# Transposing late tiles by DMA inside SBUF instead of on TensorE, with a new planned order and changed rings

## The chip, the cores and the metric

The kernel runs on 1 core of one Trainium2 chip. The metric is the device time of one execution in microseconds (us). Executions fall into a fast and a slow state; ratios and the conclusions from them use fast runs only, while a median with its range takes in the slow ones too. A ratio is the mean time of one kernel's fast runs over that of the other's of the same rounds on the same chip, so it is not quite the ratio of the medians quoted beside it. An interval after a ratio is its 95% interval. The kernel before has its own spread from chip to chip: its medians were 174.7 to 176.2 us.

## The reference, cut to what matters

```python
# attention: B=4, H=8, S=768, D=48
for t in range(S):
    cur = einsum('bhd,bhe->bhde', u[None] * kt, vt)
    y[:, :, t] = einsum('bhd,bhde->bhe', rt, state + cur)
    state = wt[..., None] * state + einsum('bhd,bhe->bhde', kt, vt)
x = y.transpose(0, 2, 1, 3).reshape(B, S, H * D)          # 4 x 768 x 384
# token mixing and a channel step
theta = x @ w_theta
y = w_tok_r @ (x * cos(theta)) + w_tok_i @ (x * sin(theta))
u = x + y
return u + maximum(u @ w_ch, 0)
```

A tile is 128 tokens of 384 channels. There are 24, numbered 0 to 23, six for each batch. Both `x @ w_theta` and `u @ w_ch` take the tile transposed (x^T, u^T), as the operand `lhsT` of TensorE's matmul.

## The kernel before

A planner orders all operations ahead of the run. It gives each operation an engine, a guessed duration and a priority, places them one by one, and so fixes the instruction stream of each engine. SP is the queue that issues the DMAs. What holds it delays every issue behind: below, the last load goes out at 142.42 us instead of 120.18. SBUF is the memory on the chip, PSUM the one that TensorE writes to. A ring is the number of buffers that the tiles of one name go through in turn.

```python
LAG = {"PE": 0.21, "ACT": 0.16, "DVE": 0.14, "POOL": 0.10, "SP": 1.5, "WQ": 2.5, "-": 0.0}
...
            for i, (eng, dur, fn, pen) in enumerate(o.alts):     # Planner.place
                t = max(free_at.get(eng, 0.0), t_slot)
                for d in o.deps:
                    t = max(t, d.end + (LAG[d.eng] if d.eng != eng else 0.0))
                if eng == "SP" and self.loads > 0:
                    t = max([free_at.get(eng, 0.0), t_slot and t_slot + self.slack[0]]
                            + [d.end + LAG[d.eng] + self.slack[1] for d in o.deps])
```

The end of a tile: TensorE mixes tokens, VectorE adds x, TensorE transposes u in three pieces into PSUM, ScalarE or VectorE copies u^T to SBUF, TensorE multiplies by `w_ch`, VectorE finishes, and SP stores.

```python
def f_ut():
    for j in range(NJ):                                   # NJ = 3
        nc.tensor.transpose(get(tx)[:, j, :], get(un)[:, j * L:(j + 1) * L], ident)
o_ut = P.op("PE", 0.17, f_ut, [o_un], [tx, uT], [], prio=-1.0, name=f"ut{b}{ti}")
...
o_uc = P.op("ACT", 0.38, f_uc, [o_ut], [], [tx], prio=-1.0, name=f"uc{b}{ti}",
            alts=[("DVE", 0.26, f_uc_v, PEN)])            # copy PSUM -> SBUF
def f_ml():
    for j in range(NJ):
        nc.tensor.matmul(get(ml), lhsT=get(uT)[:, j, :], rhs=wch[:, j, :], ...)
```

x^T is made in the same way. All loads and all output stores are issued on the SP queue.

## Time and profile before

| | |
|---|---|
| time | 174.72 us median (174.18 to 178.64, 3 runs) |
| profiled execution | span 175.3 us, state slow |
| TensorE (PE) busy in the span | 91% |
| TensorE busy from 128.6 to 171.9 us | 42.09 of 43.30 us |
| SP held by one 192 KB store | 0.34 us |

The prediction below shows how the page and its tables are read.

### The profile page before, as it was taken

The page shows a single profiled execution, that of the slowest core. Times are in us where ns is not written, and L with a number is a line of the kernel's source. Part 1 is how long each engine was busy: PE and PEld are TensorE (multiplying, and loading weights), DVE is VectorE, ACT ScalarE, POOL GpSimd, SP SyncE. Part 2 cuts the span into 40 slices and gives each one's busy share as a digit, 9 for nine tenths or more (in the row PEclk, how much of TensorE's full clock was granted, in tenths as well). Part 3 has the DMA queues.
Part 4 walks back from the last instruction along what each step waited for, and adds up shares of the span by engine and source line. Part 5 has one row for each costly group of instructions (what it writes and reads, how often), then busy time and mean ns, then how long its engine had stood idle before and what let it go on. Part 6 is the DMA issues. An engine that isn't in the chain of part 4 may idle for free.

```text
span 175.3 us, 4898 instructions
## 1 busy us (share of the span) xinstructions
PE 158.7 (91%) x1919; PEld 104.7 (60%) x1919; DVE 130.5 (74%) x278; ACT 117.7 (67%) x255; POOL 114.0 (65%) x134
## 2 busy tenths in 40 slices
PE   7699898999759999999977999999899999999980
PEld 7257565776536566776643667666566666566640
DVE  4507869797996899867899399869989884645461
ACT  2469689799996987966988049799986924810000
POOL 7388689989759578559799987999789310000000
PEclk9858699999996999999996599999999999999999
DMA  5999998899999999999999979989011012112212
GB/s 115 272 301 264 215 222 203 218 264 238 262 222 256 284 160 309 211 208 197 214 206 192 189 129 199 204 174 217 12 45 46 9 38 76 62 45 90 95 45 90
DMA packets 93768, 29.81 MB, mean 170 GB/s; under 512 B 88369, under 2 KB 92210, under 8 KB 93746
## 3 DMA queue, kind: packets, MB, share of 16 engines
q1 hardware_dynamic: 93344, 29.50, 75.9%
q8 instruction: 15, 0.25, 0.6%
q10 hardware_dynamic: 402, 0.00, 0.1%
q14 instruction: 7, 0.06, 0.1%
HBM read 24.78 MB, written 4.72 MB: 168 GB/s over the span
## 4 chain that ended last, share of the span: by engine, by line
PE 63%; DVE 12%; ACT 12%; DMA 8%; issue 1%; SPq 0%; ACTq 0%; DVEq 0%
PE bank L914 24%; DVE sb_z L891 7%; PE bank L941 6%; DMA sb_w<-in_moe_w_tok_i_dram 4%; PE cum L646 3%; PE bank L877 3%; DMA in_k<-in_k_dram 2%; DMA in_w<-in_w_dram 2%; PE bank L928 2%; PE bank L509 2%; PE bank L572 2%; ACT sb_a L439 2%; PE bank L491 2%; PE bank L493 2%; PE cum L430 2%; PE bank L593 1%
## 5 line engine op out<-in xcount | busy, mean ns | idle before, releaser
L914 PE MATMUL bank<-sb_z,wtokT 128*128 128x384 bf16 x288 | 56.3, 337 | 0.4 <-DVE sb_z L891 0.4
L914 PEld LDWEIGHTS <-wtokT 128*128 128x128 bf16 x288 | 27.2, 100 | 17.5 <-issue 3.2
L485 POOL TENSOR_TENSOR sb_bon<-sb_v,sb_rub 128x384 bf16<-128x384 bf16 x18 | 14.9, 829 | 15.0 <-ACT sb_v L465 8.4
L891 DVE TENSOR_TENSOR sb_z<-x_all,sb_sc 128x768 bf16<-128x768 bf16 x24 | 21.6, 911 | 2.4 <-ACT sb_sc L885 2.4
L923 DVE TENSOR_TENSOR sb_un<-bank,x_all 128x384 bf16<-128x384 f32 x24 | 13.3, 555 | 12.2 <-PE bank L914 12.1
L452 POOL TENSOR_TENSOR sb_k<-in_k,sb_a 128x384 bf16<-128x384 f32 x18 | 19.2, 1069 | 4.7 <-DMA in_k<-in_k_dram 4.7
L476 POOL TENSOR_TENSOR sb_ruk<-sb_ru,in_k 128x384 bf16<-128x384 f32 x18 | 19.2, 1067 | 0.6
L458 POOL TENSOR_TENSOR sb_q<-in_r,sb_a 128x384 bf16<-128x384 f32 x18 | 19.0, 1055 | 0.9 <-DMA in_r<-in_r_dram 0.9
L469 POOL TENSOR_TENSOR sb_ru<-in_r,u_bc 128x384 f32<-128x384 f32 x18 | 18.9, 1051 | 0.0
L439 ACT ACTIVATE sb_a<-cum 128x768 f32<-128x768 f32 x18 | 14.6, 810 | 6.0 <-PE cum L434 5.7
L326 ACT ACT_TABLE_LOAD x12 | 15.4, 1283 | 1.5 <-PEq L1025 1.3
L941 PE MATMUL bank<-wch,sb_uT 128*128 128x384 bf16 x72 | 15.7, 326 | 0.6 <-DVE sb_uT L935 0.6
L946 DVE SCALAR_TENSOR_TENSOR sb_o<-bank,sb_un 128x384 f32<-128x384 f32 x24 | 13.3, 553 | 3.9 <-PE bank L941 3.9
L882 ACT ACTIVATE sb_sc<-bank 128x384 bf16<-128x384 f32 x24 | 12.2, 510 | 4.1 <-PE bank L877 4.1
L932 ACT ACTIVATE sb_uT<-bank 128x384 bf16<-128x384 bf16 x16 | 7.8, 489 | 10.3 <-PE bank L928 10.1
L885 ACT ACTIVATE sb_sc<-bank,hpi 128x384 bf16<-128x384 f32 x24 | 14.6, 607 | 0.0
L877 PE MATMUL bank<-wth,sb_xT 128*128 128x384 bf16 x72 | 14.0, 326 | 0.4 <-DVE x_all L841 0.4
L497 DVE COPY sb_qkt<-bank 128x1024 bf16<-128x1024 bf16 x18 | 12.3, 683 | 1.3 <-PE bank L493 1.1
L514 DVE TENSOR_TENSOR sb_p<-bank,mask_exc 128x512 bf16<-128x512 f32 x18 | 12.3, 681 | 0.9 <-PE bank L509 0.8
L521 DVE TENSOR_TENSOR sb_p<-bank,mask_exc 128x512 bf16<-128x512 f32 x18 | 12.2, 679 | 0.0
L587 DVE TENSOR_TENSOR x_all<-bank,sb_bon 128x192 bf16<-128x192 f32 x36 | 10.9, 346 | 1.3 <-PE bank L572 1.3
L597 ACT ACTIVATE sb_xT<-bank 128x384 bf16<-128x384 bf16 x18 | 8.8, 495 | 4.3 <-PE bank L593 4.2
(131 smaller groups left out, 337.1 us busy)
## 6 DMA issues: line engine op xcount, KB each, us to landing
out_dram<-sb_o SPq DMA_DIRECT2D x24, 192.0 KB, 2.0
in_w<-in_w_dram SPq DMA_DIRECT2D x18, 192.0 KB, 5.3
in_r<-in_r_dram SPq DMA_DIRECT2D x18, 192.0 KB, 4.5
in_k<-in_k_dram SPq DMA_DIRECT2D x18, 192.0 KB, 4.5
in_v<-in_v_dram SPq DMA_DIRECT2D x18, 192.0 KB, 4.6
sb_w<-in_moe_w_tok_r_dram SPq DMA_DIRECT2D x6, 384.0 KB, 4.7
sb_w<-in_moe_w_tok_i_dram SPq DMA_DIRECT2D x6, 384.0 KB, 5.1
in_w<-in_w_dram SPq DMA_DIRECT2D x3, 384.0 KB, 5.1
```

Source lines behind the costliest of these rows:

```text
L326: nc.scalar.preload_act_table_set(name)
L439: nc.scalar.activation(get(a), get(cum)[:, :, :DM], AF.Exp)
L452: nc.gpsimd.tensor_tensor(get(kk)[:, :, :D], s["x_k"](), av(1), op=ALU.mult)
L458: nc.gpsimd.tensor_tensor(get(q)[:, :, :D], s["x_r"](), av(0), op=ALU.mult)
L469: nc.gpsimd.tensor_tensor(get(ru), s["x_r"](), u_bc, op=ALU.mult)
L476: nc.gpsimd.tensor_tensor(get(ruk), get(ru), s["x_k"](), op=ALU.mult)
L485: nc.gpsimd.tensor_tensor(get(bon), get(vb), get(rub).to_broadcast([L, H, D]), op=ALU.mult)
L877: nc.tensor.matmul(get(th), lhsT=get(s["xT"])[:, j, :], rhs=wth[:, j, :], start=(j == 0), stop=(j == NJ - 1))
L885: nc.scalar.activation(get(sc)[:, 0, :], get(th), AF.Sin, bias=hpi)
L891: nc.vector.tensor_tensor(get(zb[b])[:, c], xb, get(sc), op=ALU.mult)
L914: nc.tensor.matmul(get(ac), lhsT=wtokT[:, q_, s_, ti, :], rhs=get(zb[b])[:, s_, q_, :], start=(s_ == 0 and q_ == 0), stop=(s_ == NCH - 1 a ...
L941: nc.tensor.matmul(get(ml), lhsT=get(uT)[:, j, :], rhs=wch[:, j, :], start=(j == 0), stop=(j == NJ - 1))
```

## The change

The intent: TensorE alone sets the end, so take work from it. Six late x tiles (16 to 21) and eleven late u tiles (11 to 21) are transposed by DMA from SBUF to SBUF. That removes 51 transposes from TensorE and 17 copies from PSUM. Priorities and allocation penalties of the planner were retuned for it, and a few guessed durations changed.

```diff
+    XBAR = (11, 22)          # u tiles transposed by DMA
+    XBARX = (16, 22)         # x tiles
-    SLACK = (4.32, 5.23)
+    SLACK = (0.0, 5.53)
-    WIN = {'PE': 0.0, 'ACT': 0.0, 'DVE': 0.05, 'POOL': 0.56, 'SP': 0.12}
+    WIN = {'PE': 0.0, 'ACT': 0.02, 'DVE': 0.0, 'POOL': 0.19, 'SP': 0.0}
-             ... "sb_xT": 9, ... "sb_un": 3, "sb_uT": 3, ...
+             ... "sb_xT": 7, ... "sb_un": 4, "sb_uT": 4, ...
+        def f_ux():
+            for j in range(NJ):
+                nc.sync.dma_start(out=get(uT)[:, j, :], in_=get(un)[:, j * L:(j + 1) * L], transpose=True)
+        if XBAR[0] <= b * NCH + ti < XBAR[1]:
+            o_uc = P.op("SP", 0.9, f_ux, [o_un], [uT], [], prio=-1.0, name=f"ux{b}{ti}")
+        else:
+            (TensorE transpose and copy, as before)
     (the same for x^T with XBARX; planner durations: paired loads 1.46 -> 1.6, one state
      update 0.45 -> 0.76; the tables SHIFT and PENALTY, some 240 numbers, retuned: cut)
```

The planner takes three transposing DMAs for 0.9 us of SP and 1.5 us more until the data can be used.

More of the change, by code (lines that the diff above doesn't have):

```diff
@@ L59, in key @@
         num = name[len(kind):]
-        if kind in ("tok", "un", "ut", "uc", "ml", "fin", "st"):
+        if kind in ("tok", "un", "ut", "ux", "uc", "ml", "fin", "st"):
             b = int(num[0])
@@ L212 @@
     OFF = {'ln': -2.2, 'cum': -2.1, 'exp': -2.05, 'alt': -2.04, 'q': -1.5, 'k': -1.45, 'v': -1.2, 'ru': -1.3, 'ruk': -1.2, 'rub': -1.2, 'bon': -1.1, 'tqk': -0.9, 'qkt': -0.9, 'p': -0.8, 'm0': -0.7, 'pc': -0.7, 'sel': -1.6, 'y': -0.5, 'x': -0.5, 'xt': -0.4, 'xc': -0.4, 'rk': -1.3, 'rkt': -1.2, 'rkc': -1.2, 'beta': -1.15}
-    SHIFT = {'M': -0.23, 'M@0': 3.78, 'M@1': -3.52, 'M@3': 2.56, 'Mp@0': 0.29, 'S': -3.32, 'S@0': 0.3, 'S@1': -2.09, 'S@3': -3.9, 'Sp@0': -0.07, 'alt': -2.71, 'alt@0': -4.19, 'alt@1': -3.75, 'alt@3': -2.44, 'bc@0': -2.12, 'beta@0': 8.49, 'bon': -7.28, 'bon@0': -7.76, 'bon@1': -1.33, 'bon@3': -11.03, 'cos': -4.6, 'cos@0': -7.82, 'cos@1': -5.2, 'cos@3': -5.64, 'cum': 2.98, 'cum@0': -0.21, 'cum@1': 2.19, 'cum@3': 3.61, 'cump@0': -0.23, 'cwch': 2.19, 'cwch@1': 2.56, 'cwt': -0.63, 'cwt@1': -2.08, 'cwth': 0.26, 'cwth@1': -8.48, 'exp': -7.56, 'exp@0': -11.22, 'exp@1': -7.11, 'exp@3': -1.28, 'fin': 10.83, 'fin@0': 12.05, 'fin@1': 12.34, 'fin@3': 8.58, 'k': -2.66, 'k@0': -15.07, 'k@1': -5.34, 'k@3': -4.01, 'ldk': -0.07, 'ldk@0': 0.25, 'ldk@1': 0.06, 'ldk@3': 0.13, 'ldkp@0': -0.61, 'ldr': -0.52, 'ldr@0': -1.79, 'ldr@1': -0.84, 'ldr@3': -1.05, 'ldrp@0': -1.69, 'ldv': 0.27, 'ldv@0': 0.93, 'ldv@1': 1.13, 'ldv@3': 0.9, 'ldvp@0': 0.88, 'ldw': -1.63, 'ldw@0': -1.67, 'ldw@1': -1.98, 'ldw@3': -0.9, 'ldwp@0': -1.18, 'ln': -1.02, 'ln@0': -1.74, 'ln@1': -4.09, 'ln@3': 1.93, 'm': 1.57, 'm@0': 7.07, 'm@1': 11.91, 'm@3': 13.16, 'ml': 3.16, 'ml@0': -7.78, 'ml@1': -6.19, 'ml@3': -6.65, 'p': 4.22, 'p@0': 8.66, 'p@1': 14.26, 'p@3': 6.5, 'pc': 1.07, 'pc@0': 1.12, 'pc@1': -2.22, 'pc@3': -4.15, 'pp@0': 1.14, 'q': -0.33, 'q@0': -3.4, 'q@1': 0.28, 'q@3': 1.27, 'qkt': 1.93, 'qkt@0': -0.14, 'qkt@1': -5.68, 'qkt@3': -3.58, 'qktp@0': 2.71, 'rk@0': 6.13, 'rkc@0': 2.62, 'rkt@0': -1.07, 'ru': -2.75, 'ru@1': -1.4, 'ru@3': 2.61, 'rub': 1.54, 'rub@1': 3.53, 'rub@3': 6.25, 'ruk': -0.11, 'ruk@1': -0.56, 'ruk@3': 0.5, 'sel': 1.06, 'sel@0': 2.59, 'sel@1': -6.63, 'sel@3': -2.52, 'sin': 1.45, 'sin@0': 4.46, 'sin@1': -0.21, 'sin@3': 0.97, 'st': 0.43, 'st@0': -0.77, 'st@1': 3.72, 'st@3': -4.86, 'th': -5.14, 'th@0': -12.99, 'th@1': -9.62, 'th@3': -9.38, 'toE': -2.74, 'toE@0': -6.59, 'toE@1': -1.75, 'toE@3': -1.04, 'toS': -2.78, 'toS@0': 7.44, 'toS@1': 3.52, 'toS@3': 2.77, 'tok': -3.84, 'tok@0': -5.7, 'tok@1': -7.33, 'tok@3': -2.77, 'tqk': -0.37, 'tqk@0': -8.63, 'tqk@1': -1.82, 'tqk@3': -1.42, 'ubc': 3.86, 'ubc@1': 2.43, 'ublk@1': 8.43, 'ubm': 3.03, 'ubm@1': 3.71, 'uc': -4.81, 'uc@0': 3.89, 'uc@1': -2.11, 'uc@3': 5.25, 'un': 2.42, 'un@0': 2.75, 'un@1': -2.25, 'un@3': -1.11, 'ut': -3.32, 'ut@0': -2.56, 'ut@1': -8.44, 'ut@3': -9.24, 'v': 1.33, 'v@0': 5.45, 'v@1': 5.64, 'v@3': 6.18, 'wch': -0.56, 'wch@1': 1.93, 'wev': 2.67, 'wev@1': 6.99, 'wt': 0.86, 'wt@1': 0.73, 'wth': 0.4, 'wth@1': -1.64, 'wtr': 0.92, 'wtr@1': 2.77, 'x': 1.16, 'x@0': -4.58, 'x@1': 1.61, 'x@3': 1.76, 'xc': 1.62, 'xc@0': 2.07, 'xc@1': 3.0, 'xc@3': 1.78, 'xp@0': -0.04, 'xt': 0.48, 'xt@0': 1.96, 'xt@1': 3.17, 'xt@3': 6.63, 'y': -0.38, 'y@0': -2.78, 'y@1': -0.45, 'y@3': 0.21, 'yp@0': 1.15, 'z': -1.82, 'z@0': -4.53, 'z@1': -8.37, 'z@3': -5.1}
@@ L214 @@
-    PENALTY = {'S': 1.09, 'S@0': 1.12, 'S@1': 0.03, 'S@3': -0.59, 'bc@0': -1.6, 'bon@0': 0.89, 'cwch': -1.71, 'cwch@1': -0.3, 'cwt': 1.34, 'cwt@1': 1.64, 'cwth': 1.85, 'cwth@1': 2.85, 'k': 9.17, 'k@0': 6.71, 'k@1': 5.59, 'k@3': 6.89, 'pc': -1.22, 'pc@0': -2.79, 'pc@1': -4.83, 'pc@3': -6.18, 'qkt': 3.99, 'qkt@0': 1.6, 'qkt@1': 0.86, 'qkt@3': 2.34, 'qktp@0': 0.89, 'rk@0': 10.81, 'rkc@0': 2.27, 'ruk': -1.87, 'ruk@1': -3.89, 'ruk@3': -10.16, 'uc': 1.64, 'uc@0': 0.25, 'uc@1': 4.42, 'uc@3': -1.02, 'wev': -0.04, 'wev@1': 0.23, 'xc': -0.05, 'xc@0': 2.57, 'xc@1': 2.52, 'xc@3': 3.03, 'xp@0': 0.65}
+    SHIFT = {'M': -0.23, 'M@0': 3.78, 'M@1': -2.52, 'M@3': 3.01, 'Mp@0': 1.53, 'S': -3.32, 'S@0': 0.3, 'S@1': 0.63, 'S@3': -4.36, 'Sp@0': 1.4, 'alt': -2.71, 'alt@0': -4.47, 'alt@1': -1.63, 'alt@3': -4.6, 'bc@0': -1.23, 'beta@0': 12.08, 'bon': -7.28, 'bon@0': -5.29, 'bon@1': 0.35, 'bon@3': -8.1, 'cos': -4.6, 'cos@0': -9.33, 'cos@1': -3.49, 'cos@3': -3.96, 'cum': 2.98, 'cum@0': -0.21, 'cum@1': 3.75, 'cum@3': 5.42, 'cump@0': -1.49, 'cwch': 2.19, 'cwch@1': -0.96, 'cwt': -0.63, 'cwt@1': -3.12, 'cwth': 0.26, 'cwth@1': -9.29, 'exp': -7.56, 'exp@0': -10.19, 'exp@1': -4.56, 'exp@3': -1.55, 'fin': 10.83, 'fin@0': 10.99, 'fin@1': 9.97, 'fin@3': 7.33, 'k': -2.66, 'k@0': -18.8, 'k@1': -7.79, 'k@3': -6.46, 'ldk': -0.07, 'ldk@0': 0.25, 'ldk@1': 0.06, 'ldk@3': 0.42, 'ldkp@0': -0.45, 'ldr': -0.52, 'ldr@0': -1.79, 'ldr@1': -0.84, 'ldr@3': 0.67, 'ldrp@0': -0.91, 'ldv': 0.27, 'ldv@0': 0.93, 'ldv@1': 0.84, 'ldv@3': -0.27, 'ldvp@0': 0.3, 'ldw': -1.63, 'ldw@0': -1.67, 'ldw@1': -1.84, 'ldw@3': -0.9, 'ldwp@0': -1.25, 'ln': -1.02, 'ln@0': -1.36, 'ln@1': -1.33, 'ln@3': 6.49, 'm': 1.57, 'm@0': -0.46, 'm@1': 6.1, 'm@3': 7.68, 'ml': 3.16, 'ml@0': -6.91, 'ml@1': -8.02, 'ml@3': -8.42, 'p': 4.22, 'p@0': 8.66, 'p@1': 11.81, 'p@3': 4.5, 'pc': 1.07, 'pc@0': 1.12, 'pc@1': 0.19, 'pc@3': -5.32, 'pp@0': 1.11, 'q': -0.33, 'q@0': -4.36, 'q@1': -1.61, 'q@3': -1.63, 'qkt': 1.93, 'qkt@0': -0.16, 'qkt@1': -6.64, 'qkt@3': -4.47, 'qktp@0': 8.5, 'rk@0': 11.67, 'rkc@0': 2.6, 'rkt@0': 1.02, 'ru': -2.75, 'ru@1': 0.09, 'ru@3': 7.17, 'rub': 1.54, 'rub@1': 2.55, 'rub@3': 4.18, 'ruk': -0.11, 'ruk@1': -0.64, 'ruk@3': 0.54, 'sel': 1.06, 'sel@0': 2.59, 'sel@1': -8.51, 'sel@3': -0.48, 'sin': 1.45, 'sin@0': 8.03, 'sin@1': 7.28, 'sin@3': 7.7, 'st': 0.43, 'st@0': -3.12, 'st@1': -2.28, 'st@3': -8.52, 'th': -5.14, 'th@0': -11.38, 'th@1': -7.14, 'th@3': -9.55, 'toE': -2.74, 'toE@0': -3.59, 'toE@1': 4.98, 'toE@3': 1.37, 'toS': -2.78, 'toS@0': 8.07, 'toS@1': 9.18, 'toS@3': 4.18, 'tok': -3.84, 'tok@0': -3.56, 'tok@1': -5.9, 'tok@3': 0.22, 'tqk': -0.37, 'tqk@0': -7.79, 'tqk@1': -1.84, 'tqk@3': 1.63, 'ubc': 3.86, 'ubc@1': 2.17, 'ublk@1': 10.04, 'ubm': 3.03, 'ubm@1': -2.15, 'uc': -4.81, 'uc@0': 1.88, 'uc@1': -0.32, 'uc@3': 4.71, 'un': 2.42, 'un@0': 3.54, 'un@1': 0.59, 'un@3': 0.94, 'ut': -3.32, 'ut@0': 4.0, 'ut@1': -0.49, 'ut@3': -4.37, 'ux@1': 2.07, 'ux@3': 1.0, 'v': 1.33, 'v@0': 12.47, 'v@1': 13.27, 'v@3': 11.66, 'wch': -0.56, 'wch@1': 1.75, 'wev': 2.67, 'wev@1': 12.33, 'wt': 0.86, 'wt@1': 0.73, 'wth': 0.4, 'wth@1': -1.92, 'wtr': 0.92, 'wtr@1': 3.27, 'x': 1.16, 'x@0': -4.58, 'x@1': 1.58, 'x@3': 0.02, 'xc': 1.62, 'xc@0': 1.0, 'xc@1': 2.04, 'xc@3': -0.4, 'xp@0': -2.67, 'xt': 0.48, 'xt@0': 1.66, 'xt@1': 2.11, 'xt@3': 8.81, 'y': -0.38, 'y@0': -2.78, 'y@1': -1.02, 'y@3': -2.05, 'yp@0': 0.2, 'z': -1.82, 'z@0': 0.57, 'z@1': -4.1, 'z@3': -7.66}
@@ new lines @@
+    PENALTY = {'S': 1.09, 'S@0': 1.12, 'S@1': 0.25, 'S@3': -0.21, 'bc@0': -2.77, 'bon@0': 0.35, 'cwch': -1.71, 'cwch@1': -0.6, 'cwt': 1.34, 'cwt@1': 4.81, 'cwth': 1.85, 'cwth@1': 1.65, 'k': 9.17, 'k@0': 8.13, 'k@1': 8.89, 'k@3': 8.64, 'pc': -1.22, 'pc@0': -2.79, 'pc@1': -6.94, 'pc@3': -12.31, 'qkt': 3.99, 'qkt@0': 0.86, 'qkt@1': 3.26, 'qkt@3': 5.89, 'qktp@0': -1.33, 'rk@0': 9.44, 'rkc@0': 1.39, 'ruk': -1.87, 'ruk@1': -1.91, 'ruk@3': -13.18, 'uc': 1.64, 'uc@0': 1.43, 'uc@1': 5.04, 'uc@3': -1.26, 'wev': -0.04, 'wev@1': -0.16, 'xc': -0.05, 'xc@0': 2.47, 'xc@1': 2.67, 'xc@3': 2.65, 'xp@0': 0.98}
@@ L241 @@
              "sb_a": 3, "sb_alt": 5, "sb_v": 5, "sb_ru": 2, "sb_ruk": 2, "sb_rk": 2, "sb_rkT": 2, "beta": 1, "sb_rub": 2,
-             "sb_bon": 4, "sb_qkt": 4, "sb_p": 3, "sb_S": 3, "sb_SD": 3, "sb_xT": 9, "sb_sc": 3,
-             "sb_z": 3, "sb_w": 3, "sb_wn": 4, "sb_un": 3, "sb_uT": 3, "sb_o": 6}
+             "sb_bon": 4, "sb_qkt": 4, "sb_p": 3, "sb_S": 3, "sb_SD": 3, "sb_xT": 7, "sb_sc": 3,
+             "sb_z": 3, "sb_w": 3, "sb_wn": 4, "sb_un": 4, "sb_uT": 4, "sb_o": 6}
     cpool = ctx.enter_context(tc.tile_pool(name="cpool", bufs=1))
@@ L371, in fn @@
                               in_=src[b, :, c * L:(c + 2) * L, :].rearrange("h (p k) d -> p h (k d)", k=2))
-        o = P.op("SP", 1.46, fn, alloc=bf, prio=2 * m_ - (WAHEAD if name == "w" else 0.0), name=f"ld{name}p{2 * m_}")
+        o = P.op("SP", 1.6, fn, alloc=bf, prio=2 * m_ - (WAHEAD if name == "w" else 0.0), name=f"ld{name}p{2 * m_}")
         for k2 in range(2):
@@ L593, in f_xt @@
                 nc.tensor.transpose(t[:, j, :], x_all[:, b, c, j * L:(j + 1) * L], ident)
-        o_xt = P.op("PE", 0.17, f_xt, [o_x], [tx, xT], [], prio=pr + OFF["xt"], name=f"xt{n}")
         def f_xc():
@@ L600, in f_xc_v, with f_xx @@
             nc.vector.tensor_copy(get(xT), get(tx))
-        s["o_xc"] = P.op("ACT", 0.38, f_xc, [o_xt], [], [tx], prio=pr + OFF["xc"], name=f"xc{n}",
-                         alts=[("DVE", 0.26, f_xc_v, PEN)])
+        def f_xx():
+            for j in range(NJ):
+                nc.sync.dma_start(out=get(xT)[:, j, :], in_=x_all[:, b, c, j * L:(j + 1) * L], transpose=True)
+        if XBARX[0] <= n < XBARX[1]:
+            s["o_xc"] = P.op("SP", 0.9, f_xx, [o_x], [xT], [], prio=pr + OFF["xt"], name=f"xx{n}")
+        else:
+            o_xt = P.op("PE", 0.17, f_xt, [o_x], [tx, xT], [], prio=pr + OFF["xt"], name=f"xt{n}")
+            s["o_xc"] = P.op("ACT", 0.38, f_xc, [o_xt], [], [tx], prio=pr + OFF["xc"], name=f"xc{n}",
+                             alts=[("DVE", 0.26, f_xc_v, PEN)])
         s["o_x"] = o_x
@@ L820, in f_S @@
                                                 get(alt[g])[rows].to_broadcast([DP, NP, D]), op=ALU.mult)
-                s["o_S"] = P.op("DVE", 0.45, f_S, [o_mm, s["o_alt"]], [], [m, alt[g]], prio=pr - 0.6, name=f"Sp{n}")
+                s["o_S"] = P.op("DVE", 0.76, f_S, [o_mm, s["o_alt"]], [], [m, alt[g]], prio=pr - 0.6, name=f"Sp{n}")
             def f_y(g=g, c=c, hs=hs, ys=ys, prev=prev):
@@ L928, in f_ut @@
                 nc.tensor.transpose(get(tx)[:, j, :], get(un)[:, j * L:(j + 1) * L], ident)
-        o_ut = P.op("PE", 0.17, f_ut, [o_un], [tx, uT], [], prio=-1.0, name=f"ut{b}{ti}")
         def f_uc():
@@ L935, in f_uc_v @@
             nc.vector.tensor_copy(get(uT), get(tx))
-        o_uc = P.op("ACT", 0.38, f_uc, [o_ut], [], [tx], prio=-1.0, name=f"uc{b}{ti}",
-                    alts=[("DVE", 0.26, f_uc_v, PEN)])
+        def f_ux():
+            for j in range(NJ):
+                nc.sync.dma_start(out=get(uT)[:, j, :], in_=get(un)[:, j * L:(j + 1) * L], transpose=True)
+        if XBAR[0] <= b * NCH + ti < XBAR[1]:
+            o_uc = P.op("SP", 0.9, f_ux, [o_un], [uT], [], prio=-1.0, name=f"ux{b}{ti}")
+        else:
+            o_ut = P.op("PE", 0.17, f_ut, [o_un], [tx, uT], [], prio=-1.0, name=f"ut{b}{ti}")
+            o_uc = P.op("ACT", 0.38, f_uc, [o_ut], [], [tx], prio=-1.0, name=f"uc{b}{ti}",
+                        alts=[("DVE", 0.26, f_uc_v, PEN)])
         def f_ml():
```

## The prediction

> **What bounds the kernel now.** I read the page first (shares, then the 40 slices), then a table of busy time by stretch, then the timeline of the end, then the queue of DMA issues. The runs agree at 174.18 and 174.72 us; 178.64 is the slow state, and the profiled execution (span 175.3, time 177.04) is called slow too, so I use the profile for durations and order and 174.5 us as the base. From the page, the shares and the slices:
>
> ```profile
> PE 158.7 (91%) x1919; PEld 104.7 (60%) x1919; DVE 130.5 (74%) x278; ACT 117.7 (67%) x255; POOL 114.0 (65%) x134
> ...
> PE   7699898999759999999977999999899999999980
> ...
> DVE  4507869797996899867899399869989884645461
> ACT  2469689799996987966988049799986924810000
> ...
> PEclk9858699999996999999996599999999999999999
> DMA  5999998899999999999999979989011012112212
> ```
>
> One slice is 4.4 us. Up to slice 28 (about 120 us) the DMA row is full and PE has holes. From slice 29 the DMA row is nearly empty, PE is full, its clock is full, and ACT and DVE have room. The table by stretch says the same in microseconds (stretch, length, busy time and records per engine, clock, DMA share, GB/s):
>
> ```profile
> 80.00:100.00 20.00, 17.30 (x169) 10.41 (x168) 15.81 (x30) 14.39 (x31) 18.83 (x20) 0.83 1.08 201
> 100.00:120.00 20.00, 20.00 (x270) 13.57 (x269) 17.28 (x36) 15.50 (x39) 17.66 (x19) 1.00 0.98 179
> ...
> 115.00:128.60 13.60, 12.46 (x150) 8.31 (x148) 13.12 (x23) 13.21 (x33) 11.78 (x11) 1.00 0.53 118
> 128.60:171.90 43.30, 42.09 (x383) 26.47 (x376) 28.54 (x59) 17.31 (x37) 9.42 (x11) 1.00 0.17 60
> ```
>
> Three regimes: loads and mixed engines to 115 us; DVE (13.12 of 13.60 us) and ACT (13.21) from 115 to 128.6; **TensorE alone** from 128.6 to the end, 42.09 of 43.30 us. What leaves PE in the last regime comes off the end almost one for one. One tile's round there, from the timeline (start, length, engine, line):
>
> ```profile
> 160.08 0.33 PE L928 MATMUL bank<-ident,sb_un 128*128 128x128 bf16 x3
> 160.19 0.80 PEld L914 LDWEIGHTS <-wtokT 128*128 128x128 bf16 x6
> 160.24 1.14 PE L914 MATMUL bank<-sb_z,wtokT 128*128 128x384 bf16 x6
> 160.44 0.36 DVE L935 COPY sb_uT<-bank 128x384 bf16<-128x384 bf16 x1 [0.58 <-PE bank L928]
> 161.06 0.42 PEld L941 LDWEIGHTS <-sb_uT 128*128 128x128 bf16 x3
> 161.22 0.65 PE L941 MATMUL bank<-wch,sb_uT 128*128 128x384 bf16 x3
> ```
>
> Lengths overlap because matmuls are pipelined, so I take differences of starts. Three transposes: 160.08 to 160.24, **0.16 us**, not the 0.33 us of their records. Six mixing matmuls: 160.24 to 161.22, 0.98 us, or 0.163 us each. The copy out of PSUM is on DVE and hidden behind those six.
>
> The new work goes to the SP queue. Its current small job, a store of an output tile (ns min/median/max of its issue, then from issue to landing):
>
> ```profile
> L950 SPq DMA_DIRECT2D out_dram<-sb_o x24: 332/344/1176, 65.5 to 171.9; - x24
> ...
> DMA to landing us min/median/max: 1.8/2.0/5.1
> ```
>
> SP is held 0.34 us per issue, and the data has landed 2.0 us after it. The 5.1 us are of the time when the DMA row is full.
>
> **What the Trainium skill says.** (1) VectorE: DVE Perf Modes, section The three transpose paths: a full 128x128 bf16 transpose takes 390 ns on TensorE, into PSUM, and 1309 ns through the DMA crossbar, into SBUF. The trace has 219 ns for a TensorE record and 0.16 us for three in a stream, so in this kernel TensorE is much cheaper than the page's isolated figure; no run yet shows the crossbar. (2) Advanced Engine Details and Errata, section X-Bar Transpose (TRN2): transposing DMAs are as fast as ordinary ones; two streams of them must not be in flight together. All here are on the SP queue, so the second point is kept; the first is not shown yet. (3) DMA: Bandwidth & Descriptors, section Anatomy of one DMA: about 2 us per DMA are fixed and mostly completion (stated for the GpSimd path). The store's 2.0 us on SP agrees.
>
> **The change part by part.**
> Transposes leave PE for u tiles 11 to 21 (11 tiles) and x tiles 16 to 21 (6): 17 tiles, 51 transposes. In the stretch 128.6 to 171.9 the old kernel has 39 u transposes and 15 x transposes, that is 13 and 5 tiles; the last two u tiles stay on TensorE, so 16 of the 17 lie in the TensorE regime. 17 x 0.16 = **2.7 us** off PE, nearly all of it on the path that sets the end.
>
> Copies out of PSUM leave too. From the two instruction streams: x copies on ACT 18 to 12, u copies on ACT 16 to 11 and on DVE 8 to 2. At 0.49 us (ACT) and 0.36 us (DVE) that is 5.4 and 2.2 us. In the last regime these were hidden. The few before 128.6 may shorten the DVE and ACT stretch; against that, three evacuations of transposed weights move from ACT to DVE. I count zero for both.
>
> DMA gets 51 issues of 32 KB on the one queue that also holds loads and stores. If an issue costs SP what a store's does, a tile holds SP 3 x 0.34 = 1.0 us and its last part lands 0.7 + 2.0 = 2.7 us after the first issue. Bytes are no matter (1.7 MB beside 29.8), and from 128.6 the queue is 17% busy.[...]
>
> Is 2.7 us hidden? In the new TensorE stream the last u tiles (18 to 21) have, between their last mixing matmul and the matmuls that need u^T: 24, 18, 12+6 and 9+12 matmuls, or 3.9, 2.9, 2.9 and 3.4 us. Needed: a hand-over and the u addition, 0.2 + 0.56 us (rows above, from 160.24+0.98 to the addition at 161.42 lasting 0.56), then 2.7, together about 3.5 us; tiles 19 and 20 also wait for SP. So stalls of some 0.5 us each at two tiles, perhaps less as the first stall shifts the next. Estimate: **+0.6 us** in all.
>
> The x transposes begin among the last dozen loads, where the DMA row is full and a wait for x on the in-order SP queue holds the loads behind it. The planner now keeps 5.53 us of slack instead of 5.23 for such issues. I count 0 on average, with a tail to the bad side.
>
> The new order and rings (x^T 9 to 7, u and u^T 3 to 4) are the part I can't cost. The old holes are 2.7 us of idle PE in 80 to 100, with a clock of 0.83, and 3.4 us in 40 to 60. A new order may close or open some: 0 with +-1.5 us.
>
> Sum: 174.5 - 2.7 + 0.6 = 172.4; I write 172.3.
>
> **Rivals.**
> A. *The crossbar is serial at the page's 1309 ns.* Then a tile takes 3.9 us, the four last ones 15.7 us where TensorE's work leaves about 8: +8 us in the tail, time 178 to 182. For it: the page's figure and its remark that the hardware queue generates transposes less well. Against it: the same page calls them as fast as other DMAs, and a 192 KB store lands in 2.0 us altogether, so 1309 ns reads like a latency, of which three overlap. About 1 in 8; halfway to it (0.6 us per transpose) is 173 to 176.
> B. *Transposes hold the last loads back.* DMA is at 0.98 to 1.08 of its share up to 120 us. A transpose that waits for DVE ahead of a load, or lands in 5 us like a load, delays the last attention tiles; each microsecond there moves the start of the TensorE regime. Time 173 to 175. For it: 5.1 us maximum landing. Against it: the order was planned round it.
> C. *Hidden anyway.* If DVE or ACT, not PE, bounded the end, 2.7 us would buy nothing: 174.5. Against it: the PE row is 9 from slice 29 to 38, with 28.54 us of DVE in 43.30.
> D. *The new order is also better in the middle*, which a change that retunes every priority is made for: 169 to 171.
>
> **Range and chances.** Pipelined transposes with little stall (A and B false) put the time at 170 to 173: about two in three, a bit over half of that below 171.0, which is 2% under 174.5. B or half of A, 173 to 176, about one in five; A in full about one in eight. So faster 0.37, same 0.48, slower 0.15, and 169.3 to 176.8 us as the range.
>
> **What would show it.** PE records fall by 51 to 1868 (if the warm-up stays); PE stays above 95% busy from about 128 us to the end. Transposing issues hold SP near 0.35 us each and land in 2 to 3 us; if they hold 1 us or land in 4, A is right. Waits of PE on u^T by DMA: below 1.5 us in total. The last load lands near 120 us; if it lands later by over 2 us, B. If PE gets holes after 128 us on DVE or ACT, C. If the stretch before 115 us shortens by over 1.5 us, D. The prediction is wrong most likely through A, or through the order D, which I didn't cost.

## More of the kernel before

One more view is needed later, the SP queue at the end of the loads (start, length, engine, line, operation, count):

```profile
119.71 0.38 SPq L349 DMA_DIRECT2D in_k<-in_k_dram  x1
120.18 0.66 SPq L349 DMA_DIRECT2D in_v<-in_v_dram  x1
128.19 44.07 SPq L950 DMA_DIRECT2D out_dram<-sb_o  x14
```

The last load is issued at 120.18 us. After it, SP has 14 stores to issue in 44 us, so it looks idle.

## The result, and the profile after

The changed kernel is correct and takes **211.03 us** median (209.22 to 214.87, 4 runs); the kernel before in those rounds 176.13 us (174.18 to 178.64). The ratio is 1.206, 95% interval 1.191 to 1.222. The prediction of 172.3 us missed by 39 us.

The page of the profile after (a fast run, span 208.9 us), the lines that answer to those of before:

```profile
PE 166.4 (80%) x1868; PEld 102.3 (49%) x1868; DVE 124.4 (60%) x272; ACT 118.4 (57%) x263; POOL 110.4 (53%) x132
...
PE   7798597969797999999999994866553987782692
...
PEclk9999759996999999999999999997965899997579
DMA  5999999297999999999999354753121312211142
```

One slice is now 5.2 us. TensorE has exactly 51 records fewer, as planned, but from slice 25 (it begins at 125 us) its row is full of holes, and its granted clock falls in some of them. The table by stretch, same columns as in the prediction:

```profile
100.00:120.00 20.00, 19.62 (x277) 13.22 (x274) 17.20 (x37) 14.43 (x39) 19.14 (x21) 1.00 0.95 175
...
140.00:160.00 20.00, 10.35 (x73) 4.50 (x71) 6.91 (x13) 5.63 (x9) 6.70 (x7) 0.75 0.24 52
160.00:180.00 20.00, 15.70 (x108) 8.31 (x107) 8.26 (x17) 4.93 (x9) 0.00 (x0) 0.91 0.22 61
```

From 100 to 120 us TensorE is nearly as busy as before (19.62 against 20.00 us). From 140 to 160 us it works 10.35 of 20 us, and every other engine less. DMA is at 0.24: its 16 engines are mostly idle too. The SP queue, from the timeline of the kernel after:

```profile
113.72 4.26 SPq L604 DMA_TRANSPOSE sb_xT<-x_all  x3
...
137.43 0.52 SPq L964 DMA_DIRECT2D out_dram<-sb_o  x1
138.05 0.38 SPq L351 DMA_DIRECT2D in_k<-in_k_dram  x1
138.53 3.84 SPq L945 DMA_TRANSPOSE sb_uT<-sb_un  x3
142.42 0.58 SPq L351 DMA_DIRECT2D in_r<-in_r_dram  x1
143.10 4.78 SPq L604 DMA_TRANSPOSE sb_xT<-x_all  x3
147.99 3.71 SPq L945 DMA_TRANSPOSE sb_uT<-sb_un  x3
...
183.34 15.11 SPq L945 DMA_TRANSPOSE sb_uT<-sb_un  x12
```

Here is the queue that I took for idle. Three transposes hold it 3.7 to 4.8 us, twelve hold it 15.11 us, that is 1.26 us each. The last load is issued at 142.42 us instead of 120.18. The line's own view gives the length of one issue (min/median/max ns) and the time from the start of the issue to landing:

```profile
L945 SPq DMA_TRANSPOSE sb_uT<-sb_un x33: 1095/1222/1746, 138.5 to 197.2; - x33
...
DMA to landing us min/median/max: 2.2/2.3/3.8
```

**One issue holds SP 1.22 us**; 51 of them hold it some 64 us (51 x 1.26). The landing, 2.3 us, is close to what the prediction used. And TensorE near the end, from its timeline; a bracket gives the idle time before and what ended it:

```profile
188.17 0.34 PE L955 MATMUL bank<-wch,sb_uT 128*128 128x384 bf16 x1 [0.96 <-DMA sb_uT<-sb_un]
189.41 0.34 PE L955 MATMUL bank<-wch,sb_uT 128*128 128x384 bf16 x1 [0.91 <-DMA sb_uT<-sb_un]
190.72 0.34 PE L955 MATMUL bank<-wch,sb_uT 128*128 128x384 bf16 x1 [0.97 <-DMA sb_uT<-sb_un]
192.03 0.50 PE L955 MATMUL bank<-wch,sb_uT 128*128 128x384 bf16 x1 [0.97 <-DMA sb_uT<-sb_un]
```

TensorE does one matmul each 1.24 to 1.31 us, at the pace at which SP issues.

### The profile page after: what moved, and what is told of

Its sections match the earlier page's. It is cut to its first block, busy times and chain, and to the rows that moved or that the text cites. A ratio compares the mean times of both kernels' runs of the same rounds, so it can differ in the third digit from the quotient of the medians.

```text
span 208.9 us, 4886 instructions
## 1 busy us (share of the span) xinstructions
PE 166.4 (80%) x1868; PEld 102.3 (49%) x1868; DVE 124.4 (60%) x272; ACT 118.4 (57%) x263; POOL 110.4 (53%) x132
## 4 chain that ended last, share of the span: by engine, by line
PE 42%; SPq 20%; ACT 12%; DVE 9%; DMA 7%; issue 5%; POOL 4%; DVEq 0%; POOLq 0%; ACTq 0%
PE bank L922 15%; SPq L945 13%; SPq L604 6%; PE cum L654 4%; PE bank L955 4%; DMA sb_uT<-sb_un 3%; DVE sb_z L899 2%; DMA in_w<-in_w_dram 2%; ACT sb_sc L893 2%; ACT sb_bon L743 2%; PE bank L885 2%; PE bank L511 2%; ACT sb_S L557 1%; DMA in_v<-in_v_dram 1%; ACT sb_sc L890 1%
## 5 line engine op out<-in xcount | busy, mean ns | idle before, releaser
L955 PE MATMUL bank<-wch,sb_uT 128*128 128x384 bf16 x72 | 20.9, 357 | 21.0 <-DMA sb_uT<-sb_un 20.4
L922 PEld LDWEIGHTS <-wtokT 128*128 128x128 bf16 x288 | 27.8, 102 | 20.0 <-issue 5.6
L460 POOL TENSOR_TENSOR sb_q<-in_r,sb_a 128x384 bf16<-128x384 f32 x18 | 18.3, 1017 | 17.0 <-DMA in_r<-in_r_dram 9.9
L955 PEld LDWEIGHTS <-sb_uT 128*128 128x128 bf16 x72 | 6.6, 100 | 30.9 <-DMA sb_uT<-sb_un 28.0
L899 DVE TENSOR_TENSOR sb_z<-x_all,sb_sc 128x768 bf16<-128x768 bf16 x24 | 17.3, 735 | 6.3 <-ACT sb_sc L893 6.1
L487 POOL TENSOR_TENSOR sb_bon<-sb_v,sb_rub 128x384 bf16<-128x384 bf16 x18 | 15.8, 876 | 9.1 <-DVE sb_rub L483 6.4
L454 POOL TENSOR_TENSOR sb_k<-in_k,sb_a 128x384 bf16<-128x384 f32 x18 | 18.3, 1017 | 2.3 <-DVE x_all L589 2.1
L885 PE MATMUL bank<-wth,sb_xT 128*128 128x384 bf16 x72 | 15.6, 357 | 0.4 <-ACT sb_sc L893 0.4
L597 ACT ACTIVATE sb_xT<-bank 128x384 bf16<-128x384 bf16 x12 | 6.0, 500 | 16.1 <-PE bank L595 16.0
L516 DVE TENSOR_TENSOR sb_p<-bank,mask_exc 128x512 bf16<-128x512 f32 x18 | 12.3, 683 | 1.5 <-PE bank L511 1.4
L680 POOL TENSOR_TENSOR sb_q<-in_r,sb_a 128x384 bf16<-128x384 f32 x6 | 6.0, 997 | 12.4 <-ACT sb_alt L672 10.8
```

What stands on the lines that cost most here:

```text
L454: nc.gpsimd.tensor_tensor(get(kk)[:, :, :D], s["x_k"](), av(1), op=ALU.mult)
L460: nc.gpsimd.tensor_tensor(get(q)[:, :, :D], s["x_r"](), av(0), op=ALU.mult)
L487: nc.gpsimd.tensor_tensor(get(bon), get(vb), get(rub).to_broadcast([L, H, D]), op=ALU.mult)
L885: nc.tensor.matmul(get(th), lhsT=get(s["xT"])[:, j, :], rhs=wth[:, j, :], start=(j == 0), stop=(j == NJ - 1))
L899: nc.vector.tensor_tensor(get(zb[b])[:, c], xb, get(sc), op=ALU.mult)
L922: nc.tensor.matmul(get(ac), lhsT=wtokT[:, q_, s_, ti, :], rhs=get(zb[b])[:, s_, q_, :], start=(s_ == 0 and q_ == 0), stop=(s_ == NCH - 1 a ...
```

## The experiments

Theory T: the issue of a transposing DMA holds the in-order SP queue 1.22 us, and that makes the loss. Rivals: O, the new order and rings are at fault; L, the landing time is at fault, not the issue; later, contention of the DMAs' own work. Eighteen kernels were run, each with the kernel before on one chip.

### The order without DMA, and plain copies in place of transposes

The first puts all 17 tiles back on TensorE and keeps the rest of the change:

```diff
-    XBAR = (11, 22)
-    XBARX = (16, 22)
+    XBAR = (24, 24)
+    XBARX = (24, 24)
```

> The change with all 17 tiles back on TensorE; new priorities, ring sizes and planner durations kept. Theory T (the transposing issue holds the SP queue 1.22 us and that alone costs the 35 us): 172 to 177 us, no worse than before. Rival O (the new order and rings are what went wrong): above 185 us.

Measured: 182.28 us median (179.37 to 184.89), ratio 1.028 (1.022 to 1.035). It falls between the two expectations: the order itself costs some 5 us (2.8% of 175), which theory T did not have, but it is not the 35 us.

The second keeps the changed kernel's order and takes only the transposing away, so its result is wrong:

```diff
-  nc.sync.dma_start(out=get(uT)[:, j, :], in_=get(un)[:, j * L:(j + 1) * L], transpose=True)
+  nc.sync.dma_start(out=get(uT)[:, j, :], in_=get(un)[:, j * L:(j + 1) * L])
```

> The change with its exact order and waits, but each transposing DMA is a plain DMA copy of the same 128x128 piece (wrong result on purpose). Theory T: an issue costs about 0.35 us as for a store, a tile 1.05 us, as the prediction assumed; 170 to 175 us. Rival L (the landing time of 2.3 us after the issue, which a plain copy has nearly too, is what TensorE waits for): above 185 us. Rival O: above 185 us.

Measured: 183.6 us (182.78 to 185.42), ratio 1.053 (1.045 to 1.061). The time falls by 27 us, yet not to 170 to 175. The line's view:

```profile
L945 SPq DMA_DIRECT2D sb_uT<-sb_un x33: 464/594/657, 134.1 to 172.1; - x33
...
DMA to landing us min/median/max: 1.7/1.8/3.0
```

Even a plain copy of such a piece inside SBUF holds SP 0.59 us, not the 0.34 us of the big store to HBM that I had taken as the model. So three copies are 1.8 us, and the assumption of the prediction was not reproduced even here. The early clock of this run was low as well (0.53 from 20 to 40 us), so I draw no finer conclusion from it than this: with the same order and the same number of DMAs, the transposing makes some 27 us (ratio 1.206 to 1.053).

### One issue of 128x384 per tile

```diff
-            for j in range(NJ):
-                nc.sync.dma_start(out=get(uT)[:, j, :], in_=get(un)[:, j * L:(j + 1) * L], transpose=True)
+            nc.sync.dma_start(out=get(uT), in_=get(un), transpose=True)
```

> The change with one transposing DMA of 128x384 per tile in place of three of 128x128; result right. If the 1.22 us are a cost per issue: SP is held some 1.2 us per tile, 20 us in all, and the time is 171 to 177 us. If they are a cost per 128x128 block: one issue holds SP about 3.5 us and the time stays at 203 to 211 us.

Measured: correct, 177.99 us (175.94 to 178.47), ratio 1.017 (1.007 to 1.026). Its profile for this line:

```profile
L943 SPq DMA_TRANSPOSE sb_uT<-sb_un x11: 1179/1195/1334, 131.1 to 164.2; - x11
...
DMA to landing us min/median/max: 2.3/2.3/4.0
```

**Three times the columns take the same issue and the same landing.** At these two sizes the cost is one per issue. The time drops by 33 us, to what the order costs by itself (1.028) or a little less. Rival L falls: the landing is 2.3 us in both.

### The old order with the same DMAs

The kernel before, with its own priorities, rings and durations, and the 17 tiles by three DMAs each (edit: only the DMA branch of the change put into the kernel before).

> The kernel before (its priorities, ring sizes and planner durations) with the same 17 tiles transposed by DMA. Theory T: 200 to 215 us, as bad as the change. Rival O: below 185 us, since the order is the old one.

Measured: correct, 206.42 us (205.38 to 208.01), ratio 1.183 (1.174 to 1.192). As theory T expects; rival O can't explain this.

The same old order with one DMA per tile:

> The kernel before (its priorities, rings, planner durations) with the same 17 tiles transposed by one DMA of 128x384 each. Theory T, now that an issue costs 1.2 us whatever its columns up to 384: 172 to 176 us, and 3 to 5 us below the same issues in the new order, which was 178. If transposing DMAs cost something beside their issues (contention, landing), 177 us or more.

Measured: 175.67 us (175.49 to 176.22), ratio 1.006 (1.001 to 1.010). 31 us are back, but the gain that I had predicted is not there. The expected gap of 3 to 5 us to the same issues in the new order is 2.3 us.

### Where the predicted gain went

I then told the planner a truer cost: SP held 1.2 us, and 2.4 us more until the data may be used. (I first read the landing as counted from the end of the issue; it counts from the start, so this plan has 1.3 us in hand: 1.2 + 2.4 against 2.3.)

```diff
-   o_uc = P.op("SP", 0.9, f_ux, [o_un], [uT], [], ...)
+   o_uc = P.op("SP", 1.2, f_ux, [o_un], [uT], [], ...)
+   o_uc.lag = 2.4                      # used instead of LAG["SP"]; the same for x
```

> As the old order with one issue per tile, but the planner is told what was measured: SP held 1.2 us, landing 2.4 us after it. TensorE should wait less for u^T than in the version planned with 0.9 and 1.5: 171 to 175 us.

Measured: 174.26 us (173.01 to 175.06), ratio 0.997 (0.990 to 1.004): within noise of the kernel before. With only the u tiles by DMA:

> As the version with the measured cost told to the planner, but only the 11 u tiles go by DMA, after the loads; the 6 x tiles stay on TensorE. If the x transposes among the last loads cost more than the 6 x 0.16 us that they save: 0.5 to 2 us below the version with both. If not: equal or 1 us above it. 171 to 175 us.

Measured: 175.72 us (175.31 to 176.49), ratio 1.007 (1.002 to 1.012). So the x tiles by DMA do no harm once they cost one issue each, and probably gain about 1 us; the two intervals just touch.

Then a plan with 3.4 us for u^T (x^T keeps 2.4), and the rings of the change (x^T 7, u and u^T 4). This planned time from the end of an issue to the use of its data is called lead below:

```diff
-            o_uc.lag = 2.4
+            o_uc.lag = 3.4
-             ... "sb_xT": 9, ... "sb_un": 3, "sb_uT": 3, ...
+             ... "sb_xT": 7, ... "sb_un": 4, "sb_uT": 4, ...
```

> Old order with one issue per tile, u rings 4 and x^T ring 7 as in the change, and the planner told 3.4 us to landing, 1 us of it as margin. If the wait of TensorE for u^T (3 us in the version with 2.4 us) is what eats the 2.7 us: that wait falls below 1.5 us and the time is 171.5 to 173.5 us. If the waits only move: 174 to 175.5 us.

Measured: correct, 171.13 us (169.57 to 173.65), ratio 0.965 (0.954 to 0.976), faster than both kernels. Two of its four runs were slow, so it was repeated with its relatives, five rounds each on one chip:

> The same kernel as the old order with more lead, on another chip beside its nearest relatives. If its gain is real: 0.955 to 0.98 of the kernel before. If it was that chip's noise: 0.985 to 1.0.

> That kernel with the planner told 2.4 us to landing, as measured, in place of 3.4; rings kept (x^T 7, u and u^T 4). If the margin of 1 us is what hides the wait for u^T: 1.5 to 3 us above it, near the version with the old rings. If the larger u rings are what helped: equal to it within 1 us.

> The version with old rings and 2.4 us again, now beside the others on one chip: 0.985 to 1.005 of the kernel before, and 1.5 to 4 us above the version with more lead.

| version (old order, one issue per tile) | median us (range) | ratio (interval) |
|---|---|---|
| rings 9/3/3, lead 2.4 | 174.08 (172.31 to 175.94) | 0.988 (0.981 to 0.995) |
| rings 7/4/4, lead 2.4 | 171.85 (171.31 to 172.64) | 0.980 (0.975 to 0.985) |
| rings 7/4/4, lead 3.4 | 171.48 (169.56 to 173.61) | 0.974 (0.967 to 0.981) |

The gain is real, 2.6% or 4.5 us on this chip, though the interval does not say whether it is over 2%. Between the rows, the fast runs differ by 0.8% or 1.5 us for the rings and by 0.6% or 1 us for the extra lead; the intervals of neighbouring rows overlap, so neither share is certain, and the 1.5 to 3 us from the margin did not come. No run has the rings 7/4/4 with the transposes left on TensorE, so what they bring without DMA is not shown. What moved with them is the wait of TensorE for u^T. First the version with the old rings, waits of TensorE by line (us in total, times, longest; PEld is its weight load, and the two overlap):

```profile
PEld L956 <- DMA sb_uT<-sb_un: 2.3, 3, 1.0
PE bank L956 <- DMA sb_uT<-sb_un: 1.1, 2, 0.6
```

With the larger rings and the same lead (both profiled runs are fast ones):

```profile
PEld L956 <- DMA sb_uT<-sb_un: 1.0, 3, 0.5
```

And the version with the larger rings and more lead (its profiled run was a slow one, so only the waits are read from it):

```profile
PEld L956 <- DMA sb_uT<-sb_un: 0.7, 2, 0.5
```

### Three issues put back into the best version

All engines' orders are those of the best version; only the loop of three DMAs is back. First in all 17 tiles, then in the 6 x tiles alone, then in the 11 u tiles alone.

> That kernel with the three transposing DMAs of 128x128 per tile put back, all engines' orders the same but for the 34 added issues. Theory T (34 more issues at 1.22 us on an in-order queue): 195 to 210 us. If the DMA's own work or the order were what cost the 35 us: below 180 us.

> The best version with three issues for the 6 x tiles only (12 more issues, 15 us more of SP, among the last loads). If the 35 us come through the loads held back: more than half of them are here, 190 us or more, and the last load is issued near 145 us. If they come mainly through u^T in the tail: 172 to 182 us.

> The best version with three issues for the 11 u tiles only (22 more issues, 28 us more of SP, mostly after the loads). If the tail is limited by SP at 3.8 us per tile where TensorE needs less: 188 to 200 us. If the loads held back are the cost: below 182 us.

| three issues in | added issues | median us (range) | ratio | last load issued at |
|---|---|---|---|---|
| no tile | 0 | 171.48 (169.56 to 173.61) | 0.974 | 129.9 us (slow run) |
| the x tiles | 12 | 179.88 (179.15 to 181.28) | 1.031 | 142.6 us |
| the u tiles | 22 | 191.34 (188.94 to 193.79) | 1.094 | 131.2 us |
| all | 34 | 206.31 (206.22 to 207.62) | 1.177 | 145.2 us |

So the 34 issues cost 35 us in an order that is otherwise good, and the u tiles in the tail are the larger part of it, as the second branch of the x run's expectation and the first of the u run's have it. The middle rows come from another chip than the outer ones, so I compare ratios. In the x tiles the issues hold the loads back: the last load comes 13 us later, and the ratio rises by 0.057, 10 us. In the u tiles they slow the tail: 0.119, 21 us. The two make 31 us; the other 4 to 5 us are no more than the intervals of the two rows (1.016 to 1.047 and 1.071 to 1.117) leave open. The record's own verdict is "unclear" for all four rows; the intervals of the last two rows lie far above 1 all the same (the last: 1.169 to 1.185). Contention of the DMAs' own work would show in their landing: the 33 u issues of the last row land in 2.3 us (median, longest 3.3), the 11 of the first row in 2.3 us (longest 4.0). What the queue does in the 1.22 us is not shown, and no run issued from another queue. The waits in the version with three issues in the x tiles alone show which engines starved, in those of the u tiles alone TensorE waits for u^T instead. First the x tiles:

```profile
POOL sb_k L455 <- DMA in_k<-in_k_dram: 9.8, 3, 4.1
ACT sb_v L468 <- DMA in_v<-in_v_dram: 7.0, 2, 4.6
```

Then the u tiles:

```profile
PEld L957 <- DMA sb_uT<-sb_un: 19.4, 20, 1.3
PE bank L957 <- DMA sb_uT<-sb_un: 12.2, 16, 1.0
```

The time of the last load alone does not decide: with the rings 7/4/4 and lead 2.4 (a fast run) it is issued at 127.0 us, later than the 120.2 us of the kernel before, and the kernel is faster.

### What the new order costs by itself

The 5 us of the order without DMA showed an early loss. At the 14th tile in attention order, VectorE, GpSimd and TensorE were behind the kernel before; two candidates stood out near 20 to 40 us. One is SP waiting for a weight buffer. From the waits of the SP queue, order without DMA:

```profile
SPq L384 <- ACT sb_alt L446: 7.9, 1, 7.9
```

The other is ScalarE doing the bonus product (v times a row factor) in 8 instructions, twice in a row, which the planner takes for 1.0 us each. From its timeline (the last line is GpSimd, idle 4.26 us before):

```profile
18.21 1.91 ACT L743 ACTIVATE sb_bon<-sb_v,sb_rub 128x48 bf16<-128x48 bf16 x8
20.21 1.91 ACT L743 ACTIVATE sb_bon<-sb_v,sb_rub 128x48 bf16<-128x48 bf16 x8
...
26.07 1.00 POOL L680 TENSOR_TENSOR sb_q<-in_r,sb_a 128x384 bf16<-128x384 f32 x1 [4.26 <-ACT sb_alt L672]
```

The profile of the order without DMA is that of a slow run, but the changed kernel, in a fast one, shows both too: SP waits 6.7 us at the same load, and GpSimd is idle for 4.15 us.

The slack of loads put back (`SLACK = (4.32, 5.53)`):

> The new order without DMA transposes, with one planner number put back: 4.32 us of slack after a buffer is freed before a load is placed, in place of 0. Theory S (the new order loses its 5 us because SP waits 8 us at a weight load for a buffer near 33 us and no loads flow): the wait of SP there is under 3 us and the time 173 to 178 us. Rival (the retuned priorities lose it elsewhere): 179 to 184 us.

Measured: 178.89 us (177.08 to 179.37), ratio 1.022 (1.013 to 1.030). SP still waits 5.7 us at that load, so the number did not remove the wait, and this run neither supports nor refutes the wait as a cause.

The bonus product at its measured 1.91 us:

> The new order without DMA transposes, with one planner number corrected: the 8-instruction bonus product on ScalarE costs 1.91 us as the trace shows, not 1.0; the planner then leaves all 24 of these products to GpSimd, where the new order had put 3 on ScalarE. Theory B (these hold ScalarE near 20 us, starve GpSimd and let TensorE's clock fall): 173 to 177 us. Rival (the order loses its 5 us elsewhere): 179 us or more.

Measured: 179.04 us (176.31 to 180.66), ratio 1.006 (0.993 to 1.019) against 1.028, on another chip, with the product on ScalarE. Two of the four runs were slow; the fast ones, 176.31 and 177.94 us, lie on both sides of 177, the upper end of theory B, so it is not settled.

Both:

> Both early repairs of the new order, still without DMA transposes: bonus product at its measured 1.91 us and 4.32 us of slack for loads. Theory: the early part is as in the kernel before; 173 to 176 us. Rival: 178 us or more.

Measured: 176.71 us (172.24 to 179.09) beside 176.23 us of the kernel before; only one of four runs was fast, too few for an interval. In that run, of 172.24 us, SP waits no more than 1.8 us at one place in the early part, and GpSimd starts the 18th tile at 96.7 us. The changed kernel, also in a fast run, starts it at 104.3, before its first transposing DMA at 113.7; the slow runs of the order without DMA and of the kernel before have 109.7 and 98.8. All repairs with one issue per tile:

> The change with all that was learned: one transposing DMA per tile, planned at 1.2 us of SP and 2.4 us to landing, bonus product at 1.91 us, 4.32 us of slack. If the early part is repaired: 171 to 175 us, at or below the kernel before. If not: 177 us or more.

Measured: 178.05 us (173.73 to 180.5), again with one fast run (173.73). So the repairs bring the new order near the old one, and its loss is likely the early part, but its runs spread over 7 us and how the 5 us divide stays open.

## Why the prediction was wrong, point by point

- **What bounds the kernel** fits the runs: with the transposes gone at one issue per tile, the best version gains 4.5 us, more than the 2.7 us of the sum. It differs from the kernel before in rings and plan too, and with the old rings the gain was none (1.006) or little (0.997, repeated 0.988), so the 2.7 us alone are not shown.
- **"If an issue costs SP what a store's does, a tile holds SP 3 x 0.34 = 1.0 us"** is the step that failed. An issue holds SP 1.22 us, so a tile holds it 3.7 us, and its last part lands 2 x 1.26 + 2.3 = 4.8 us after the first issue starts, not 2.7. Two thirds of those 3.7 us are the second and third issue, which held up the loads and then u^T: without them the time fell from 206.3 to 171.5 us. The trace before had no transposing DMA, and I took the duration of another operation on the same queue.
- **"From 128.6 the queue is 17% busy"** was a misreading: 0.17 is the share of the 16 DMA engines, not of the SP queue. After the change these stayed at 0.22 to 0.24; the queue that issues was the bound. Its load was not in any row that I summed: 17 x 3.7 = 63 us in a window of some 85 us (113.7 to 198.5), beside loads and stores.
- **Rival A had the size, not the place**: it named the page's 1309 ns and a tile of 3.9 us, but a crossbar that takes this for each 128x128 block would have kept one issue of three blocks at 3.9 us, and it held SP 1.20 us. The cost is in the issue. A's chance, 1 in 8, rested on the argument that 1309 ns reads like a latency; and I let it act only on the four last tiles (+8 us). The cost acts on all 17: about 21 us by the u tiles and 10 us by loads held behind the x tiles.
- **Rival B** (loads held back) was real as part of A: the last load at 142.4 us instead of 120.2, against "lands near 120 us" in the list of signs.
- **The new order at 0 +- 1.5 us** was mis-sized: it costs about 5 us (ratio 1.028). Rival D, a better middle, was wrong.
- **Signs**: 1868 records came as said; the hold of over 1 us told in one look that the cost of a tile was wrong. TensorE's weight loads waited 28.0 us in total for u^T, against the 1.5 us of the list. Small slip: the PE row shows 8, not 9, in slice 29.
- **Stalls for u^T of 0.6 us**: with one issue, where the assumption of a short hold nearly stands, the weight loads waited 2.3 us with the old rings and 0.7 us in the best version.

## What to carry to other kernels

Before work moves to a DMA queue, count issues, not bytes: number of issues times the time one of them holds its queue, against what else must pass through that in-order queue. If no row of the trace has this operation, measure it alone first; a page's figure that looks too long deserves more than 1 in 8. Then ask for fewer, larger issues: here one transposing DMA of 128x384 costs what one of 128x128 does, and that turned 206 us into 171 us.

## What the Trainium skill lacked or had wrong

- VectorE: DVE Perf Modes, section The three transpose paths: its 1309 ns for the crossbar is near the 1.22 us that an issue holds its queue here (1.26 us from one to the next). The table does not say which time its figure is, nor that 128x384 takes no more here (1.20 us).
- Advanced Engine Details and Errata, section X-Bar Transpose (TRN2): "TRN2 transpose DMAs are as fast as regular DMAs" does not hold for single small pieces here: the plain copy of the same 32 KB of u held SP 0.59 us and landed in 1.8 us, the transposing one 1.22 and 2.3 us.
- DMA: Bandwidth & Descriptors, section Issuing engines are not separate DMA queues: it calls the sequencer's time for an issue "usually small relative to the DMA itself". For a transpose here it is 1.22 of 2.3 us, and three in a row bound the kernel.
